# Weight tiles at 128 modulo 256 bytes, weight parts formed later, and a second layer by pairs of output chunks

## The chip, the cores and the metric

The program runs on one NeuronCore of one Trainium2 chip. The metric is the device time of one execution in microseconds; three runs of the kernel before took 576.20, 577.55 and 580.22 us (median 577.55).

## What is computed

Causal attention (2 batches, 12 heads, 448 positions, 64 wide) gives x, 896 tokens by 768. A gated layer and an output layer follow, then a second pair of layers with a cosine:

```python
x = attention(q, k, v)                      # 896 x 768
x = (sigmoid(x @ w_gate) * (x @ w_val)) @ w_out     # 768 -> 1536 -> 768
h = x @ w_in                                # 768 -> 2048
return (h * cos(h)) @ w_out2                # 2048 -> 768
```

All inputs are float32. The weights arrive as 64-bit words and are turned into float32 on the chip.

## The kernel before

**Layout.** Features stand on the 128 partitions, tokens in the free dimension, 448 (one batch) to a matmul. A weight chunk is up to six blocks of 128x128, laid out as 128x768.

**Three matmuls to a block product.** Float32 operands are split in a high and a low part (type float32r): `hi` is rounded by ScalarE (ACT), `lo` is the difference, formed by VectorE (DVE). One product of a weight block with a 448-token operand is hi by high, hi by low, lo by high (L221 to L223 in `products`, L521 to L523 in the units below). From the start of the first layer to the end these are 144 + 630 + 432 + 576 + 576 = 2358 matmuls (plain products, units, second, third and fourth layer) of the one form 128x128 by 128x448.

**A chunk's way.** DMA `wraw` (two buffers), ACT rounds the top half into `up` (L157), DVE puts the words together in `wf` (L159), ACT rounds `whi` (L169, L484), DVE subtracts `wlo` (L171, L418). Each engine works off its instructions strictly in the order in which they are written; there is no scheduler.

**First layer.** The first two feature chunks (`PLAIN`) are plain products. The other ten are units of Strassen's scheme: seven block products p1 to p7 of nine matmuls each, written in the order 1, 5, 2, 6, 4, 7, 3, where 4 belongs to the unit before. (The first unit has 1, 5, 6, 2, 7, 3, the last one's 4 follows alone.) The weights of p1 and p2 are a chunk's own parts (`A`); those of p5 and p6 are the parts of sums `s12`, those of p7 and p3 of sums `s34`, that of p4 the tile `a22`. The other operands are blocks of x and the sums T1 to T4, which are formed once, during the plain products.
Between the products stand: after p1 a copy of PSUM bank a to b (L547), over which p2 must wait, since it writes on into a; after p6 the sum c = b + s5 (L562), over which p7 must wait, since it writes on into b. `emit` writes a product first and then the work after the product before it; the weight work of the next chunk follows in each turn of the loop.
In the last unit `split_h` begins to split the layer's results h into high and low (one ACT and one DVE instruction each, L226 and L227).

**Second layer and on.** For each of six output chunks m, two weight chunks c, two batches b: 18 matmuls. `advance()` splits the next chunk, decodes the one after and loads a third. Third and fourth layer are alike; the change leaves them as they are.

**Addresses.** Tiles lie in SBUF in the order in which pools are opened and tags first used. In the built program, bytes within a partition: `wraw` at 16512, `up`, two `wf`, then four `whi` from 38048 and four `wlo` from 50336, 3072 apart; all eight are 160 modulo 256. `a22` is 224 modulo 256. Every operand that streams against them (x, T, h, y, g) is 192 modulo 256. Blocks within a tile are 512 bytes (weights) or 1792 bytes (moving) apart, so the remainder is that of every matmul of its kind, or with blocks of 512 bytes its own again.

Of the kernel before, what the change touches and what calls it, by code (L numbers as in the profile page):

```python
# [9 lines left out]
F32 = mybir.dt.float32  # L10
F32R = mybir.dt.float32r
# [4 lines left out]
AF = mybir.ActivationFunctionType  # L16
# [3 lines left out]
P = 128  # L20
B, H, S, D = 2, 12, 448, 64
# [6 lines left out]
KX = DM // P  # L28
# [3 lines left out]
WC = 6  # L32
# [3 lines left out]
WH = KP * P  # L36
PLAIN = 2
# [32 lines left out]
def attn_moe_moe2(  # L70
# [9 lines left out]
    nc = tc.nc  # L80
# [2 lines left out]

    wpool = ctx.enter_context(tc.tile_pool(name="wpool", bufs=4))
    bpool = ctx.enter_context(tc.tile_pool(name="bpool", bufs=1))
    psum = ctx.enter_context(tc.tile_pool(name="psum", bufs=8, space=PSUM))

    def bank():
        return psum.tile([P, 512], F32, tag="ps", name="ps")

    def slot(tag, name, dtype=F32R):
        pool = gpool if tag[0] == "g" else spool if tag[0] == "t" else hpool if tag in ("f0", "f1", "f2") else bpool
        return pool.tile([P, 2, S], dtype, tag=tag, name=name)
# [12 lines left out]
    chunks = []  # L106
    for f in range(KH):
        chunks.append((w_gv[f, :, 0], KX))
        chunks.append((w_gv[f, :, 1], KX))
    for m in range(KX):  # L110
        for c in range(0, KH, WC):
            chunks.append((w_out[m, :, c : c + WC], WC))
    for f in range(KG):
        chunks.append((w_in2[f], KX))
    for m in range(KX):
        for c in range(0, KG, WC):
            n = min(WC, KG - c)
            chunks.append((w_out2[m, :, c : c + n], n))
    raws, singles, parts = {}, {}, {}
# [4 lines left out]
    def step(kind):  # L124
        c = at_chunk[kind]
        at_chunk[kind] = c + 1
        return c if c < len(chunks) else None
# [13 lines left out]
    class Chunk:  # L141
# [22 lines left out]
        def split(self, step, e0, e1):  # L164
            if step == 0:
                if e0 == 0:
                    self.hi = wpool.tile([P, WC * P], F32R, tag="whi", name="whi")
                    self.lo = wpool.tile([P, WC * P], F32R, tag="wlo", name="wlo")
                nc.scalar.activation(self.hi[:, e0:e1], self.w[:, e0:e1], AF.Copy)  # L169
            else:  # L170
                nc.vector.tensor_tensor(  # L171
                    self.lo[:, e0:e1], self.w[:, e0:e1], self.hi.bitcast(F32)[:, e0:e1], op=ALU.subtract
                )
                if e1 == self.n:
                    parts[self.c] = (self.hi, self.lo)
# [15 lines left out]
    def next_chunk():  # L191
        return parts.pop(step("use"))
# [15 lines left out]
    def decode_load():  # L208
        decode_chunk()
        load_chunk()  # L210

    def advance():
        split_chunk()
        decode_load()

    def products(ps, wt, rhs, first, last, ks=None):
        hi, lo = wt
        n = len(rhs)
        for k in ks or range(n):
# [9 lines left out]
    with tc.tile_pool(name="apool", bufs=1) as apool, tc.tile_pool(name="a2", bufs=2) as a2:  # L229
# [12 lines left out]
        at = {}  # L242
# [142 lines left out]
        wt = next_chunk()  # L385
        pg = [bank()]
        xr = [[XB[b][k] for k in KORD] for b in range(B)]
# [13 lines left out]
    hpool = ctx.enter_context(tc.tile_pool(name="hpool", bufs=1))  # L401
    early = ExitStack()
    epool = early.enter_context(tc.tile_pool(name="epool", bufs=1))
    epool.tile([P, 8], F32, tag="pad", name="pad")

    def temp(tag, bufs):
        return epool.tile([P, S], F32, tag=tag, name=tag, bufs=bufs)
# [9 lines left out]
    def difference(dst, a, b):  # L417
        nc.vector.tensor_tensor(dst, a, b, op=ALU.subtract)  # L418
# [19 lines left out]
    def run(n):  # L438
        for i in range(n):
            next(todo, None)  # L440
# [3 lines left out]
    def gated(f, b, sg, val):  # L444
        if HF[f] is None:
            HF[f] = slot(f"f{f}", f"h{f}", F32)
        nc.vector.tensor_tensor(HF[f][:, b], sg, val, op=ALU.mult)

    for f in range(PLAIN):
        sg = []  # L450
        if f:
            wt = next_chunk()
            pg = []
            advance()
        else:
            decode_load()
        for b in range(B):
            if f:
                pg.append(bank())
                products(pg[b], wt, xr[b], True, True)  # L460
            sg.append(temp("sg", 4))
            nc.scalar.activation(sg[b], pg[b][:, :S], AF.Sigmoid)
            run(3)
        wt = next_chunk()
        if f == PLAIN - 1:
            words = [singles[2 * PLAIN].w]
        advance()
        if f == PLAIN - 1:
            words.append(singles[2 * PLAIN + 1].w)
        for b in range(B):  # L470
            pv = bank()
            products(pv, wt, xr[b], True, True)
            gated(f, b, sg[b], pv[:, :S])
            run(3)

    class Unit:

        def __init__(self, f):
            self.f = f

        def parts(self, src):
            hi = wpool.tile([P, WC * P], F32R, tag="whi", name="whi")
            lo = wpool.tile([P, WC * P], F32R, tag="wlo", name="wlo")
            nc.scalar.activation(hi, src, AF.Copy)  # L484
            return hi, lo

# [14 lines left out]
            difference(self.s34[:, :WH], f0[:, :WH], f1[:, :WH])  # L501
            difference(self.s34[:, WH:], f0[:, WH:], self.s12[:, WH:])

        def prepare34(self):
            self.sums34()
            self.S34 = self.parts(self.s34)
            self.low(self.S34, self.s34)

        def prepare22(self):
            t = epool.tile([P, 2, WH], F32R, tag="a22", name="a22", bufs=2)  # L510
            src = self.w[1][:, WH:]
            nc.scalar.activation(t[:, 0], src, AF.Copy)
            difference(t[:, 1], src, t.bitcast(F32)[:, 0])
            self.A22 = t[:, 0], t[:, 1]

        def product(self, ps, weights, half, rhs, first, last):
            hi, lo = weights
# [26 lines left out]
        def after(self, n):  # L544
# [18 lines left out]
            else:  # L563
# [2 lines left out]
                self.tmp = temp("tmp", 2)  # L566
                nc.vector.tensor_tensor(self.tmp, self.e[:, :S], self.s5, op=ALU.add)


    HTAGS = ["t12", "t13", "t14"] + [f"{x}{i}" for x, i0 in (  # L570
        ("b", 0), ("t", 0), ("b", 3), ("t", 3), ("t", 6), ("b", 6), ("t", 9)) for i in range(i0, i0 + 3)]
# [2 lines left out]
    H = [[None] * KH for b in range(B)]  # L574

    def split_h(n):
        for i in range(n):
            if HORD:
                k, b = HORD.pop(0)
                H[b][k] = slot(HTAG.pop(0), f"h{k}{b}")  # L580
                split(H[b][k], HF[k][:, b])

    def upper_of():
        k = Chunk(step("decode"))
        k.decode(0, 0, k.n)
        return k

    def word_of(k):
        k.decode(1, 0, k.n)
        load_chunk()  # L590
        return k.w
# [3 lines left out]
    def emit(u, n):  # L595
        u.p(n)
        if done:
            v, m = done.pop()
            v.after(m)
        done.append((u, n))  # L600

    unit, old = Unit(PLAIN), None
    unit.w, unit.A = words, next_chunk()
    unit.sums12()
    unit.S12 = unit.parts(unit.s12)
    unit.low(unit.S12, unit.s12)
    for f in range(PLAIN, KH):
        new, last = Unit(f + 1), f == KH - 1
        for at, n in enumerate((1, 5, 2, 6, 4, 7, 3) if old else (1, 5, 6, 2, 7, 3)):
            emit(old if n == 4 else unit, n)  # L610
            if at == 0:
                unit.prepare34()
            elif at == 1:
                unit.prepare22()
                k0 = upper_of()
            elif at == 2:
                w0 = word_of(k0)
                new.A = unit.parts(w0)
            elif at == 3:
                unit.low(new.A, w0)  # L620
                k1 = upper_of()
            elif at == 4:
                new.w = w0, word_of(k1)
                if not last:
                    new.sums12()
            elif at == 5 and not last:
                new.S12 = new.parts(new.s12)
                new.low(new.S12, new.s12)
            run(3)
            if last and at:  # L630
                split_h(2)
        unit, old = new, unit
    emit(old, 4)
    old.after(4)
    early.close()

# [5 lines left out]
    singles[2 * KH + 1] = k1  # L642
    X2 = [[None] * KX for b in range(B)]
    nch = KH // WC
    for m in range(KX):
        ps2 = [bank(), bank()]
        for c in range(nch):
            wt = next_chunk()
            advance()
            for b in range(B):  # L650
                products(ps2[b], wt, H[b][c * WC : c * WC + WC], c == 0, c == nch - 1)
                split_h(4)
                if c == nch - 1:
                    X2[b][m] = slot(f"f{2 * m + b}", f"y{m}{b}")
                    split(X2[b][m], ps2[b][:, :S])

    def turns(ph):
        k = tpool.tile([P, S], F32, tag="t0", name="k")  # L660
# [25 lines left out]
    for f in range(KG):  # L686
        wt = next_chunk()
# [10 lines left out]
    nch = (KG + WC - 1) // WC  # L698
    for m in range(KX):
        ps2 = [bank(), bank()]  # L700
        for c in range(nch):
            wt = next_chunk()
# [71 lines left out]
```

## Time and profile before

| | us |
|---|---|
| runs, median (lowest, highest) | 577.55 (576.20, 580.22) |
| the profiled execution, device time | 578.74 |
| its span, first to last instruction | 577.0 |
| TensorE busy | 563.9 (98%) |
| VectorE, ScalarE, GpSimd busy | 336.5, 315.6, 59.2 |

TensorE (PE) carries 94% of the chain of work that ended last. Its matmuls are pipelined: each lasts about 0.37 us in the records while a new one starts every 0.20 us, so the time of a stretch is read from the distance between starts, not from the durations. The mean granted TensorE clock is 0.991 of full. Stages: attention to about 79 us, plain products to 104.6, units to 245.9, second layer to about 335, third and fourth to 573.5.

### The profile page before, as it was taken

To read this page: it belongs to the slowest core of one execution; us is meant where nothing else is said; L and a number is where in the kernel's file an instruction comes from. 1 tells how busy PE (TensorE), PEld (TensorE's weight loads), DVE (VectorE), ACT (ScalarE), POOL (GpSimd) and SP (SyncE) were. 2 spreads that over 40 slices of the span, in tenths; PEclk is the share of its full clock that TensorE was granted. 3 is DMA by queue.
4 is the path that set the end of the run, shared out by engine and by line. 5 is a ranking of instruction groups with operands and counts; after the bars stand their busy time and mean duration, and the time that the engine had idled before them with its cause. 6 is when DMAs were issued, how large, how long until landed. Compare 5 with 4: busy or idle time off the path is not lost.

```text
span 577.0 us, 8165 instructions
## 1 busy us (share of the span) xinstructions
PE 563.9 (98%) x3104; PEld 492.4 (85%) x3104; DVE 336.5 (58%) x623; ACT 315.6 (55%) x611; POOL 59.2 (10%) x131
## 2 busy tenths in 40 slices
PE   7999999899999999799999999999999999999997
PEld 5666689699999989699999999999999999999996
DVE  5889969677777676773333337777777723311310
ACT  5899865465555555563333248777777732422320
POOL 4779830000000000000000000000000000000000
PEclk9999999899999999799999999999999999999999
DMA  8655033154443333333333313333333134532500
GB/s 331 243 182 205 2 110 111 55 160 122 136 130 110 110 110 110 110 109 110 111 109 110 110 56 109 110 109 111 109 101 96 60 115 154 176 98 99 161 33 32
DMA packets 14726, 68.15 MB, mean 118 GB/s; under 512 B 1632, under 2 KB 3808, under 8 KB 14688
## 3 DMA queue, kind: packets, MB, share of 16 engines
q1 hardware_dynamic: 14400, 67.33, 35.7%
q8 instruction: 24, 0.39, 0.3%
q10 hardware_dynamic: 288, 0.31, 0.2%
q14 instruction: 14, 0.11, 0.1%
HBM read 64.88 MB, written 2.75 MB: 117 GB/s over the span
## 4 chain that ended last, share of the span: by engine, by line
PE 94%; DVE 2%; ACT 2%; POOL 1%; issue 1%; ACTq 0%; POOLq 0%
PE ps L221 21%; PE ps L223 20%; PE ps L222 20%; PE ps L521 7%; PE ps L523 7%; PE ps L522 7%; PE ps L319 4%; PE ps L335 4%; PE ps L295 3%; POOL pbuf L279 1%; ACT pbuf L303 1%; PE ps L249 1%; ACT up L157 0%; ACT h L226 0%; DVE h L227 0%
## 5 line engine op out<-in xcount | busy, mean ns | idle before, releaser
L171 DVE TENSOR_TENSOR wlo<-wf,whi 128x768 fp32r<-128x768 f32 (+2 forms) x51 | 47.3, 928 | 64.5 <-ACT whi L169 63.5
L157 ACT ACTIVATE up<-wraw 128x768 f16<-128x768 bf16 (+2 forms) x71 | 74.0, 1043 | 10.1 <-DMA wraw<-in_w_out_dram 10.1
L159 DVE SCALAR_TENSOR_TENSOR wf<-wraw,up 128x768 uint32<-128x768 uint32 (+2 forms) x71 | 66.8, 941 | 18.0 <-ACT up L157 17.2
L222 PE MATMUL ps<-y,whi 128*128 128x448 f32 x192 | 70.9, 369 | 0.0
L222 PE MATMUL ps<-g,whi 128*128 128x448 f32 x192 | 70.9, 369 | 0.0
L221 PE MATMUL ps<-y,whi 128*128 128x448 f32 x192 | 70.8, 369 | 0.0
L223 PE MATMUL ps<-y,wlo 128*128 128x448 f32 x192 | 70.8, 369 | 0.0
L221 PE MATMUL ps<-g,whi 128*128 128x448 f32 x192 | 70.8, 369 | 0.0
L223 PE MATMUL ps<-g,wlo 128*128 128x448 f32 x192 | 70.8, 369 | 0.0
L223 PE MATMUL ps<-h,wlo 128*128 128x448 f32 x144 | 53.1, 369 | 0.0
L221 PE MATMUL ps<-h,whi 128*128 128x448 f32 x144 | 53.1, 369 | 0.0
L222 PE MATMUL ps<-h,whi 128*128 128x448 f32 x144 | 53.1, 369 | 0.0
L169 ACT ACTIVATE whi<-wf 128x768 fp32r<-128x768 f32 (+2 forms) x51 | 40.9, 803 | 15.9 <-DVE wf L159 15.9
L303 ACT ACTIVATE pbuf<-ps,nm 128x64 f32<-128x64 f32 (+6 forms) x84 | 38.6, 481 | 9.5 <-DVE nm L299 8.9
L664 DVE SCALAR_TENSOR_TENSOR r<-r,k 128x448 f32<-128x448 f32 x32 | 20.0, 625 | 35.8 <-ACT r L663 34.3
L521 PE MATMUL ps<-T,whi 128*128 128x448 f32 x90 | 34.6, 385 | 5.9 <-DVE ps L562 3.5
L279 POOL TENSOR_SCALAR pbuf<-pbuf,rs 128x64 f32<-128x64 f32 (+6 forms) x84 | 39.1, 486 | 9.4 <-PE ps L295 6.3
L221 PEld LDWEIGHTS ps<-y,whi 128*128 128x128 f32 x192 | 36.1, 188 | 3.6
L223 PEld LDWEIGHTS ps<-g,wlo 128*128 128x128 f32 x192 | 36.1, 188 | 3.6
L223 PEld LDWEIGHTS ps<-y,wlo 128*128 128x128 f32 x192 | 36.1, 188 | 3.6
L221 PEld LDWEIGHTS ps<-g,whi 128*128 128x128 f32 x192 | 36.1, 188 | 3.6
L222 PEld LDWEIGHTS ps<-g,whi 128*128 128x128 f32 x192 | 36.1, 188 | 3.5
(96 smaller groups left out, 1098.5 us busy)
## 6 DMA issues: line engine op xcount, KB each, us to landing
wraw<-in_w_gv_dram SPq DMA_DIRECT2D x24, 768.0 KB, 4.3
wraw<-in_w_out_dram SPq DMA_DIRECT2D x24, 768.0 KB, 4.4
wraw<-in_w_in_dram SPq DMA_DIRECT2D x16, 768.0 KB, 4.3
qkv<-in_qkv_dram SPq DMA_DIRECT2D x9, 928.0 KB, 5.0
wraw<-in_w_out_dram SPq DMA_DIRECT2D x6, 512.0 KB, 3.8
out_dram<-o SPq DMA_DIRECT2D x11, 224.0 KB, 2.0
qkv<-in_qkv_dram SPq DMA_DIRECT2D x3, 256.0 KB, 6.1
qkv<-in_qkv_dram SPq DMA_DIRECT2D x1, 672.0 KB, 5.7
```

The source lines that it names most:

```text
L157: nc.scalar.activation(up.bitcast(F16)[:, 1::2], self.top[:, e0:e1], AF.Copy)
L159: nc.vector.scalar_tensor_tensor(self.w[:, e0:e1].bitcast(U32), self.mid[:, e0:e1], 13, up.bitcast(U32), op0=ALU.logical_shift_right, op1= ...
L169: nc.scalar.activation(self.hi[:, e0:e1], self.w[:, e0:e1], AF.Copy)
L171: nc.vector.tensor_tensor(self.lo[:, e0:e1], self.w[:, e0:e1], self.hi.bitcast(F32)[:, e0:e1], op=ALU.subtract)
L221: mm(ps[:, :S], lhsT=hi[:, blk], rhs=r[:, 0], start=first and k == 0, stop=False)
L222: mm(ps[:, :S], lhsT=hi[:, blk], rhs=r[:, 1], start=False, stop=False)
L223: mm(ps[:, :S], lhsT=lo[:, blk], rhs=r[:, 0], start=False, stop=last and k == n - 1)
L279: nc.gpsimd.tensor_scalar(row, row, rs[:, i : i + 1], 1.0, op0=ALU.mult, op1=ALU.mult)
L303: nc.scalar.activation(pb[:, POFF[i] : POFF[i] + w], ps[:, :w], AF.Exp, scale=-1.0, bias=nm[:, i : i + 1], accum_out=sums[:, i : i + 1],)
L521: mm(ps[:, :S], lhsT=hi[:, blk], rhs=r[:, 0], start=start, stop=False, skip_group_check=True)
L522: mm(ps[:, :S], lhsT=hi[:, blk], rhs=r[:, 1], start=False, stop=False, skip_group_check=True)
L523: mm(ps[:, :S], lhsT=lo[:, blk], rhs=r[:, 0], start=False, stop=stop, skip_group_check=True)
```

## The change

Three things are done, all in one function.

**Addresses.** `whi` and `wlo` are allocated first in their pool (`first` holds the pair of the first chunk), so they start at 16512 and 28800, and the pad in front of `epool` grows from 8 to 48 floats. In the built program all `whi`, `wlo` and `a22` are then 128 modulo 256; the streamed operands stay at 192, at the addresses that they had.

**Order in the units.** The sums `s12` of the first unit, and their parts, are formed inside the last plain product; in a unit the parts of a set of sums are formed one block product behind the sums, and the high part of `a22` and the decoding of the next chunk come ahead of them; the low parts of `A` and `S12` of the next unit move to the end. The last unit splits 9 instead of 12 of the 24 tiles of h.

**Second layer.** Output chunks are done in pairs: four PSUM banks, and for each batch both chunks' weights, so that the second batch is wanted two products later.

```diff
+    def weights(tag):
+        return wpool.tile([P, WC * P], F32R, tag=tag, name=tag)
+
+    first = [weights("whi"), weights("wlo")]
...
-    for m in range(KX):
+    for m in range(0, KX, 2):
         for c in range(0, KH, WC):
-            chunks.append((w_out[m, :, c : c + WC], WC))
+            for i in range(2):
+                chunks.append((w_out[m + i, :, c : c + WC], WC))
...
-    epool.tile([P, 8], F32, tag="pad", name="pad")
+    epool.tile([P, 48], F32, tag="pad", name="pad")
...
+        def high22(self):
+            self.a22 = epool.tile([P, 2, WH], F32R, tag="a22", name="a22", bufs=2)
+            nc.scalar.activation(self.a22[:, 0], self.w[1][:, WH:], AF.Copy)
+            self.A22 = self.a22[:, 0], self.a22[:, 1]
+
+        def low22(self):
+            difference(self.a22[:, 1], self.w[1][:, WH:], self.a22.bitcast(F32)[:, 0])
...
         advance()
         if f == PLAIN - 1:
-            words.append(singles[2 * PLAIN + 1].w)
+            unit = Unit(PLAIN)
+            unit.w = words + [singles[2 * PLAIN + 1].w]
+            unit.sums12()
+            unit.S12 = unit.parts(unit.s12)
         for b in range(B):
             pv = bank()
             products(pv, wt, xr[b], True, True)
-            gated(f, b, sg[b], pv[:, :S])
+            if f == PLAIN - 1 and b == 0:
+                unit.low(unit.S12, unit.s12)
             run(3)
+            gated(f, b, sg[b], pv[:, :S])
...
             emit(old if n == 4 else unit, n)
             if at == 0:
-                unit.prepare34()
+                unit.high22()
+                k0 = upper_of()
+                unit.sums34()
             elif at == 1:
-                unit.prepare22()
-                k0 = upper_of()
+                unit.S34 = unit.parts(unit.s34)
+                unit.low22()
+                w0 = word_of(k0)
             elif at == 2:
-                w0 = word_of(k0)
-                new.A = unit.parts(w0)
+                k1 = upper_of()
+                unit.low(unit.S34, unit.s34)
             elif at == 3:
-                unit.low(new.A, w0)
-                k1 = upper_of()
+                new.A = unit.parts(w0)
+                new.w = w0, word_of(k1)
             elif at == 4:
-                new.w = w0, word_of(k1)
-                if not last:
+                if last:
+                    unit.low(new.A, w0)
+                else:
                     new.sums12()
             elif at == 5 and not last:
                 new.S12 = new.parts(new.s12)
+                unit.low(new.A, w0)
+            if at == len(order) - 1 and not last:
                 new.low(new.S12, new.s12)
             run(3)
-            if last and at:
-                split_h(2)
+            if last and at > 1:
+                split_h(1 + at // 4)
         unit, old = new, unit
     emit(old, 4)
+    split_h(1)
     old.after(4)
...
-    for m in range(KX):
-        ps2 = [bank(), bank()]
+    for m in range(0, KX, 2):
+        ps2 = [[bank() for i in range(2)] for b in range(B)]
         for c in range(nch):
-            wt = next_chunk()
-            advance()
+            wts = [next_chunk()]
             for b in range(B):
-                products(ps2[b], wt, H[b][c * WC : c * WC + WC], c == 0, c == nch - 1)
-                split_h(4)
-                if c == nch - 1:
-                    X2[b][m] = slot(f"f{2 * m + b}", f"y{m}{b}")
-                    split(X2[b][m], ps2[b][:, :S])
+                advance()
+                for i in range(2):
+                    if i and not b:
+                        wts.append(next_chunk())
+                    products(ps2[b][i], wts[i], H[b][c * WC : c * WC + WC], c == 0, c == nch - 1)
+                    split_h(3)
+                    if c == nch - 1:
+                        X2[b][m + i] = slot(f"f{2 * (m + i) + b}", f"y{m + i}{b}")
+                        split(X2[b][m + i], ps2[b][i][:, :S])
```

ScalarE before the first unit and in its first products, before the change (T is a sum of x, `s12` and `s34` sums of weights, `up` the top half of a chunk, L547 the copy of bank a to b):

```order
L157 ACTIVATE up_86<-wraw_85 128x768
L226 ACTIVATE T12_1267<-xf4_83 128x448
L226 ACTIVATE T22_1270<-xf5_84 128x448
...
L226 ACTIVATE T42_1276<-xf5_84 128x448
L484 ACTIVATE whi_1472<-s12_1469 128x768
L484 ACTIVATE whi_1489<-s34_1486 128x768
L547 COPY ps_1503<-ps_1476 128x448
L512 ACTIVATE a22_1505<-wf32_1412 128x384
L157 ACTIVATE up_86<-wraw_85 128x768
```

The same place of the changed kernel, whose lines are numbered anew (L521 is the copy of a to b):

```order
L164 ACTIVATE up_88<-wraw_87 128x768
L462 ACTIVATE whi_1419<-s12_1416 128x768
L232 ACTIVATE T12_1267<-xf4_85 128x448
...
L232 ACTIVATE T42_1276<-xf5_84 128x448
L484 ACTIVATE a22_1486<-wf32_1412 128x384
L164 ACTIVATE up_88<-wraw_87 128x768
L521 COPY ps_1503<-ps_1476 128x448
L462 ACTIVATE whi_1505<-s34_1490 128x768
```

The rounding of the parts of `s12` has moved ahead of six roundings of T, and the copy of the bank ahead of the rounding of the parts of `s34`. The later units have the same turn of the copy and the `s34` rounding.

VectorE in the last unit up to the sum c (L562), before the change:

```order
L418 TENSOR_TENSOR s34_2475<-wf32_2386,s12_2431 128x384
L418 TENSOR_TENSOR wlo_2479<-s34_2475,whi_2478 128x768
L418 TENSOR_TENSOR a22_2494<-wf32_2416,a22_2494 128x384
L227 TENSOR_TENSOR h00_2499<-h0_1320,h00_2499 128x448
L227 TENSOR_TENSOR h10_2502<-h1_1435,h10_2502 128x448
L159 SCALAR_TENSOR_TENSOR wf32_2497<-wraw_85,up_86 128x768
L227 TENSOR_TENSOR h20_2521<-h2_1585,h20_2521 128x448
L227 TENSOR_TENSOR h30_2524<-h3_1696,h30_2524 128x448
L418 TENSOR_TENSOR wlo_2519<-wf32_2497,whi_2518 128x768
L227 TENSOR_TENSOR h40_2541<-h4_1807,h40_2541 128x448
L227 TENSOR_TENSOR h50_2544<-h5_1918,h50_2544 128x448
L562 TENSOR_TENSOR ps_2556<-ps_2492,s5_2514 128x448
```

And of the changed kernel, where the sum c is L536:

```order
L424 TENSOR_TENSOR s34_2479<-wf32_2366,s12_2430 128x384
L424 TENSOR_TENSOR a22_2475<-wf32_2400,a22_2475 128x384
L166 SCALAR_TENSOR_TENSOR wf32_2477<-wraw_87,up_88 128x768
L424 TENSOR_TENSOR wlo_2495<-s34_2479,whi_2494 128x768
L233 TENSOR_TENSOR h00_2514<-h0_1324,h00_2514 128x448
L166 SCALAR_TENSOR_TENSOR wf32_2511<-wraw_87,up_88 128x768
L233 TENSOR_TENSOR h10_2533<-h1_1448,h10_2533 128x448
L536 TENSOR_TENSOR ps_2545<-ps_2492,s5_2509 128x448
```

Four splits of h and one low part of weights no longer stand ahead of the sum; one putting-together of words has come ahead of it.

## Rows read from the trace of the kernel before

**Rows 1.** Timeline of PE, plain products: start us, us, engine line op out<-in count.
```profile
79.33 0.47 PE L221 MATMUL ps<-x,whi 128*128 128x448 f32 x1
...
104.64 0.36 PE L521 MATMUL ps<-x,whi 128*128 128x448 f32 x1
```

**Rows 2.** Stages: stretch, us, busy us (instructions) of each engine, granted clock, DMA.
```profile
106.20:113.90 7.70, 4.94 (x16) 3.68 (x15) 5.44 (x10) 3.78 (x6) 0.00 (x0) 0.78 0.00 0
150.20:163.20 13.00, 13.00 (x64) 11.72 (x63) 9.40 (x15) 7.17 (x12) 0.00 (x0) 1.00 0.41 123
246.00:573.00 327.00, 327.00 (x1584) 297.48 (x1583) 149.78 (x210) 158.52 (x252) 0.00 (x0) 1.00 0.32 105
```

**Rows 3.** Timeline of PE, a unit: p2 from its first matmul.
```profile
150.18 0.46 PE L521 MATMUL ps<-x,whi 128*128 128x448 f32 x1
150.47 0.36 PE L522 MATMUL ps<-x,whi 128*128 128x448 f32 x1
...
150.88 0.37 PE L521 MATMUL ps<-x,whi 128*128 128x448 f32 x1
...
151.50 0.37 PE L521 MATMUL ps<-x,whi 128*128 128x448 f32 x1
```

**Rows 4.** Timeline of PE, another unit: p2, p6, then p4, whose weights are a22.
```profile
189.65 0.36 PE L522 MATMUL ps<-x,whi 128*128 128x448 f32 x1
...
193.06 0.36 PE L521 MATMUL ps<-T,a 128*128 128x448 f32 x1
...
193.67 0.36 PE L521 MATMUL ps<-T,a 128*128 128x448 f32 x1
```

**Rows 5.** Timeline of PE, the first unit: p1's last matmul and p5.
```profile
106.24 0.37 PE L523 MATMUL ps<-x,wlo 128*128 128x448 f32 x1
109.05 0.47 PE L521 MATMUL ps<-T,whi 128*128 128x448 f32 x1 [2.45 <-ACT whi L484]
...
111.03 0.57 PE L523 MATMUL ps<-T,wlo 128*128 128x448 f32 x1
...
113.27 0.57 PE L523 MATMUL ps<-T,wlo 128*128 128x448 f32 x1
...
113.94 0.36 PE L522 MATMUL ps<-T,whi 128*128 128x448 f32 x1
```

**Rows 6.** Timeline of PE, the last unit: p4's last matmul, p7, p3.
```profile
233.87 0.36 PE L523 MATMUL ps<-T,a 128*128 128x448 f32 x1
237.69 0.74 PE L521 MATMUL ps<-T,whi 128*128 128x448 f32 x1 [3.46 <-DVE ps L562]
...
243.71 0.36 PE L522 MATMUL ps<-x,whi 128*128 128x448 f32 x1
```

**Rows 7.** Waits: who waited for whom: us in total, times, longest us.
```profile
PEld ps L521 <- ACT ps L547: 2.1, 10, 0.3
```

**Rows 8.** Timeline of ACT around the first unit's start.
```profile
99.76 2.89 ACT L226 ACTIVATE T<-xf 128x448 fp32r<-128x448 f32 x6
108.16 0.84 ACT L484 ACTIVATE whi<-s 128x768 fp32r<-128x768 f32 x1 [5.51 <-DVE s L418]
...
111.71 0.53 ACT L547 COPY ps<-ps 128x448 f32<-128x448 f32 x1
...
112.59 1.06 ACT L157 ACTIVATE up<-wraw 128x768 f16<-128x768 bf16 x1
```

**Rows 9.** Timeline of DVE around the first unit's start.
```profile
99.92 0.96 DVE L159 SCALAR_TENSOR_TENSOR wf<-wraw,up 128x768 uint32<-128x768 uint32 x1
...
105.38 1.69 DVE L227 TENSOR_TENSOR T<-xf,T 128x448 fp32r<-128x448 f32 x3
106.98 0.55 DVE L495 TENSOR_TENSOR s<-wf 128x384 f32<-128x384 f32 x1
...
109.03 0.96 DVE L418 TENSOR_TENSOR wlo<-s,whi 128x768 fp32r<-128x768 f32 x1 [0.91 <-ACT whi L484]
```

**Rows 10.** Timeline of DVE, the last unit: the sum c.
```profile
237.01 0.63 DVE L562 TENSOR_TENSOR ps<-ps,s 128x448 f32<-128x448 f32 x1
```

More of the change, by code (lines that the diff above doesn't have):

```diff
@@ L166, in split @@
                 if e0 == 0:
-                    self.hi = wpool.tile([P, WC * P], F32R, tag="whi", name="whi")
-                    self.lo = wpool.tile([P, WC * P], F32R, tag="wlo", name="wlo")
+                    self.hi, self.lo = first if self.c == 0 else (weights("whi"), weights("wlo"))
                 nc.scalar.activation(self.hi[:, e0:e1], self.w[:, e0:e1], AF.Copy)
@@ L447, in gated @@
         nc.vector.tensor_tensor(HF[f][:, b], sg, val, op=ALU.mult)
-    for f in range(PLAIN):
-        sg = []
-        if f:
-            wt = next_chunk()
-            pg = []
-            advance()
[L455 to L468, printed above, removed]
-            words.append(singles[2 * PLAIN + 1].w)
-        for b in range(B):
-            pv = bank()
-            products(pv, wt, xr[b], True, True)
-            gated(f, b, sg[b], pv[:, :S])
-            run(3)
     class Unit:
@@ L481, in parts @@
         def parts(self, src):
-            hi = wpool.tile([P, WC * P], F32R, tag="whi", name="whi")
-            lo = wpool.tile([P, WC * P], F32R, tag="wlo", name="wlo")
+            hi, lo = weights("whi"), weights("wlo")
             nc.scalar.activation(hi, src, AF.Copy)
@@ L502, in sums34 @@
             difference(self.s34[:, WH:], f0[:, WH:], self.s12[:, WH:])
[L504 to L514, printed above, removed]
+        def high22(self):
[4 more added lines that the diff above has]
+            difference(self.a22[:, 1], self.w[1][:, WH:], self.a22.bitcast(F32)[:, 0])
         def product(self, ps, weights, half, rhs, first, last):
@@ L567, in after @@
                 nc.vector.tensor_tensor(self.tmp, self.e[:, :S], self.s5, op=ALU.add)
+    for f in range(PLAIN):
+        sg = []
+        if f:
+            wt = next_chunk()
+            pg = []
+            advance()
+        else:
+            decode_load()
+        for b in range(B):
+            if f:
+                pg.append(bank())
+                products(pg[b], wt, xr[b], True, True)
+            sg.append(temp("sg", 4))
+            nc.scalar.activation(sg[b], pg[b][:, :S], AF.Sigmoid)
+            run(3)
+        wt = next_chunk()
+        if f == PLAIN - 1:
+            words = [singles[2 * PLAIN].w]
+        advance()
+        if f == PLAIN - 1:
+            unit = Unit(PLAIN)
+            unit.w = words + [singles[2 * PLAIN + 1].w]
+            unit.sums12()
+            unit.S12 = unit.parts(unit.s12)
+        for b in range(B):
+            pv = bank()
+            products(pv, wt, xr[b], True, True)
+            if f == PLAIN - 1 and b == 0:
+                unit.low(unit.S12, unit.s12)
+            run(3)
+            gated(f, b, sg[b], pv[:, :S])
     HTAGS = ["t12", "t13", "t14"] + [f"{x}{i}" for x, i0 in (
@@ L600, in emit @@
         done.append((u, n))
[L602 to L606, printed above, removed]
+    old = None
+    unit.A = next_chunk()
     for f in range(PLAIN, KH):
         new, last = Unit(f + 1), f == KH - 1
-        for at, n in enumerate((1, 5, 2, 6, 4, 7, 3) if old else (1, 5, 6, 2, 7, 3)):
+        order = (1, 5, 2, 6, 4, 7, 3) if old else (1, 5, 6, 2, 7, 3)
+        for at, n in enumerate(order):
             emit(old if n == 4 else unit, n)
             if at == 0:
-                unit.prepare34()
+                unit.high22()
+                k0 = upper_of()
+                unit.sums34()
             elif at == 1:
-                unit.prepare22()
-                k0 = upper_of()
+                unit.S34 = unit.parts(unit.s34)
+                unit.low22()
+                w0 = word_of(k0)
             elif at == 2:
-                w0 = word_of(k0)
+                k1 = upper_of()
+                unit.low(unit.S34, unit.s34)
+            elif at == 3:
                 new.A = unit.parts(w0)
-            elif at == 3:
-                unit.low(new.A, w0)
-                k1 = upper_of()
+                new.w = w0, word_of(k1)
             elif at == 4:
-                new.w = w0, word_of(k1)
-                if not last:
+                if last:
+                    unit.low(new.A, w0)
+                else:
                     new.sums12()
@@ L644, in attn_moe_moe2 @@
     nch = KH // WC
-    for m in range(KX):
-        ps2 = [bank(), bank()]
+    for m in range(0, KX, 2):
+        ps2 = [[bank() for i in range(2)] for b in range(B)]
         for c in range(nch):
-            wt = next_chunk()
-            advance()
+            wts = [next_chunk()]
             for b in range(B):
-                products(ps2[b], wt, H[b][c * WC : c * WC + WC], c == 0, c == nch - 1)
-                split_h(4)
-                if c == nch - 1:
-                    X2[b][m] = slot(f"f{2 * m + b}", f"y{m}{b}")
-                    split(X2[b][m], ps2[b][:, :S])
+                advance()
+                for i in range(2):
[6 more added lines that the diff above has]
+                        split(X2[b][m + i], ps2[b][i][:, :S])
     def turns(ph):
```

## The prediction

> **What bounds the kernel now.** PE carries 94% of the chain that ended last, so I asked what sets the distance from one matmul to the next. I read the timeline of PE by starts (durations overlap), then the stages, then what ended its few waits.
>
> All 2358 matmuls of the four layers have one form, but three paces. In the plain products 126 start between 79.33 and 104.64 [rows 1]: 25.31 us, or 0.200 us each once the first 0.3 us are taken off. In the last three layers 1584 touch the stretch of 327.0 us, two begun before it: 327.0/1582 = 0.2067 us [rows 2]. In the units both occur: after a short wait three matmuls come 0.20 apart, then 0.62 us for three [rows 3]. And at the granted half clock six take 2.24 us, 0.373 each [rows 5]. Half of that, 0.187 us, is what streaming 448 columns would take at full clock, so 13 or 20 ns of each full-speed step are not streaming.
>
> What chooses between 0.200 and 0.2067? The weights are at 160 modulo 256 in both, so the address alone doesn't. But one stretch ran at 0.200 for 17 steps (3.41 us) and changed where weights at another remainder came, a22 at 224: 0.61 us for three from there [rows 4]. The plain products kept 0.200 until the first wait. So the slow pace is entered after a wait or a change of remainder, and once entered it stays: nothing interrupts the 1582.
>
> Two long waits stand out. The first unit's p5 waits 2.45 us for the high part of the s12 weights, then the clock falls to half for a while (0.78 on average); from 106.24 to 113.94 only 14 steps are made [rows 2, 5]. In the last unit p7 waits 3.46 us for the sum c on DVE; from 233.87 to 243.71 17 steps [rows 6]. Smaller ones: p2 of each unit waits 0.1 us for the copy of its bank [rows 3, 7].
>
> **The change part by part.** From 106.24 the trace has 7.70 us (14 steps), 119.93 us (580 steps, 113.94 to 233.87), 9.84 us (17), 2.29 us (12, to 246.0) and 327.0 us (1582) [rows 2, 5, 6]: 466.8 us for 2205 steps (counted by the program's nine matmuls to a block product). I put the changed kernel against this.
>
> *The first wait.* ACT stands idle for 5.51 us before it rounds the parts of s12, because DVE reaches the sums only at 106.98, behind six low parts of T and the gates [rows 8, 9]. In the change the sums follow the words of the chunk, which are done at 100.88: sums to 102.0 (1.15 us, as 106.98 to 108.13), high part 102.9, low part 103.9. The six roundings of T follow on ACT, 2.89 us, to 105.8; on DVE three low T (1.69 us) to 105.6, one gate (about 0.6) to 106.2, three more T to 107.9, gate 108.5. PE wants p5 at 106.44: all of its weights and T1 are there. The wait is gone, and with it the half clock, which the trace shows only behind the two long waits.
>
> What is late next: s34 sums 108.5 to 109.6 on DVE, then the low part of a22 (0.55) and the next words (0.96) to 111.1, the low part of s34 to 112.1, the sum c to 112.7 with row lengths laid end to end, 112.1 where they overlap as three T in 1.69 us do. At 0.200 a product takes 1.8 us, so p7 wants bank b at 111.84. I take 0.4 us between 0.3 and 0.9. The next unit's low part of A comes up to 0.4 us late behind the same queue; I take 0.2. New waits: **0.6 us**.
>
> *The units.* The copy now stands before the rounding that waits for the s34 sums: behind a rounding for a22 (as the copy, 0.53), the upper halves (1.06) and its own 0.53 [rows 8], some 2.7 us into the unit where p2 starts at 3.6. The nine waits of 0.1 us go. DVE is busy for 9.4 of 13.0 us and ACT for 7.2 [rows 2], with the same instructions before and after, so a unit of 63 x 0.200 = 12.6 us still covers them. S12's low part, now last, ends about 0.5 us into the unit, and p5 wants it at 1.8.
>
> *The last wait.* The sum c starts at 237.01 and p7 wanted it by 234.1 [rows 6, 10]: DVE was alternating with ACT over six splits of h and two low parts. Now two splits stand ahead. Counted from the unit's start: gate 1.3, s34 2.4, a22 3.0, words 3.9, low s34 4.9, h00 6.3 (ACT rounds it after two chunk halves, 5.7), words 7.2, h10 8.2, c 8.8 against p7 at 9.0. The wait goes; if the cover fails, tenths of a microsecond come back.
>
> *The second layer by pairs.* Matmuls, bytes and instructions are the same. The splits of h that moved out of the unit are wanted after two more products, 7.2 us. What gets tighter is a pair's second chunk: its parts stand behind the last split of the pair before, 0.55 + 0.84 + 0.96 and some signalling, 3 us where 3.6 are there. Nothing, either way; SP's queue keeps its order.
>
> *The addresses.* No trace here has weights at 128. The bounds come from the rows: at best no more than streaming, 0.187; at worst I take the slow pace and one more step of its size, 0.2133. I choose 0.200: it is the fastest pace seen at full clock, it held for as long as neither a wait nor a change of remainder came, and the change takes away the change of remainder (a22 now equals the rest) and nearly all waits.
>
> The Trainium skill speaks against it: "TensorE: Matmul & The Clock Gate", on what each phase of a matmul is for, says that PE has two independent SBUF read ports, so that loading the next weights takes no bandwidth from the running matmul, and under "Back-to-back issue gap" gives 448/2.4 + 2.5 = 189 ns, an estimate by that page. By that rule an address could neither cost nor give anything. The measured 200 and 206.7 ns, and the change of pace at a22, fit it badly; that rule without its number is rival B below.
>
> *The sum.* 2205 steps at 0.200 are 441.0 us, 25.8 less than 466.8: the two waits with their half clock 4.90 and 6.44, the units 3.93 (0.9 of it the nine waits), the rest 10.6 by pace. With 0.6 of new waits 25.2 go. The profiled execution took 578.74 us (span 577.0), 1.2 above the median of the runs; 578.74 - 25.2 = 553.5, and 552.4 at the level of the median.
>
> **The rivals.**
> *B, the pace stays as it is.* The new wait of the first unit sends PE into 0.2067, as most waits in the units did, and the addresses don't bring it back: 2205 x 0.2067 = 455.7, 11.1 less, 0.6 back: 577.55 - 10.5 = **567.0**. For it: at one remainder both paces exist. A mixture ends between, near 560.
> *C, the pace falls below 0.200.* One step of 6.7 ns less on the 2339 steps from 79.33 is another 15.6 us: **536.8**; no overhead at all would be 521. For it: at half clock nothing but the stream is seen. Against it: nothing at full clock has been faster than 0.200.
> *D, slower: the new remainder is worse.* If weights at 128 collide more often with the stream at 192, at 0.2133, the time is 567.0 + 0.9 (the plain products lose their fast pace) + 15.6 = **583.5**. It decides from 0.2108 on, where 552.4 + 2339 x 0.0108 reaches the old time. For it: the remainder does move the pace [rows 4], and no row shows this one.
> *E, a new long wait.* Should one of my orders be late by what the old ones were, 4.9 to 6.4 us come back: about 558 on top of my forecast, 573 on top of B. Against it: the margins above fall short by tenths at most.
>
> **How the numbers follow.** My forecast 0.45, B with mixtures 0.28, C 0.17, D 0.06, E 0.04. The time is that of the likeliest, 552.4. The range reaches to C's first step and to B: 535 to 569; outside stay D, the rest of C and part of E, under 2 in 10. The likeliest case alone spans 550 to 555. About 1%, 5.8 us, is what a measurement can tell from no change: faster by more (under 571.8) 0.89, within 0.06, slower 0.05.
>
> **What would show it.** In the profile after: steps of 0.200 from 79 us to the end, and 316 us for 1582 of them; no half clock behind p5 of the first unit or p7 of the last; p2 starting without a pause; DVE's sum c of the last unit ending before p7 is due. Steps of 0.2067 in the second layer would make me wrong by B, 0.193 by C, 0.213 by D; a new idle stretch of microseconds by E.

## The result, and the profile after

The changed kernel took **553.5 us** (median of 4 runs, 553.38 to 553.67) against 577.83 us (4 runs, 576.20 to 580.22) of the kernel before: a ratio of 0.9576, 95% interval 0.9542 to 0.9610. Forecast were 552.4 us, range 535 to 569. The profiled execution took 553.42 us, 25.3 us less than that of the kernel before; 25.2 were forecast.

The page of the changed kernel, its span and two of its parts: busy us (share) and instructions of PE, and the granted clock in 40 slices of the span.

```profile
span 551.6 us, 8156 instructions
...
PE 544.9 (99%) x3104; PEld 488.4 (89%) x3104; DVE 334.4 (61%) x623; ACT 315.1 (57%) x611; POOL 59.2 (11%) x131
...
PEclk9999999999999999999999999999999999999999
```

PE is busy for 19 us less with the same 3104 instructions, and no slice of the clock stands below 9. The stages, with the columns of [rows 2]:

```profile
106.20:113.90 7.70, 7.70 (x39) 6.92 (x38) 7.54 (x13) 4.70 (x7) 0.00 (x0) 1.00 0.32 98
113.90:233.80 119.90, 119.90 (x599) 111.86 (x599) 92.19 (x140) 74.29 (x117) 0.00 (x0) 1.00 0.40 126
...
250.00:540.00 290.00, 290.00 (x1452) 271.88 (x1451) 137.24 (x191) 147.01 (x233) 0.00 (x0) 1.00 0.33 109
```

In the first line, where the kernel before had 16 matmuls at a mean clock of 0.78, there are 39 at full clock. In the last, 1452 matmuls touch 290.0 us, two of them begun before it: 290.0/1450 = 0.2000 us a step, against 0.2067 in the same layers before.

The timeline of PE shows where the changed kernel still waits (start us, us, engine line op out<-in count; p7 of the first unit, p1 of the second, p4 of the last):

```profile
79.17 0.47 PE L227 MATMUL ps<-x,whi 128*128 128x448 f32 x1
...
111.49 0.37 PE L497 MATMUL ps<-x,wlo 128*128 128x448 f32 x1
111.82 0.47 PE L495 MATMUL ps<-T,whi 128*128 128x448 f32 x1
...
115.73 0.37 PE L496 MATMUL ps<-x,whi 128*128 128x448 f32 x1
116.03 0.47 PE L497 MATMUL ps<-x,wlo 128*128 128x448 f32 x1
...
116.74 0.36 PE L497 MATMUL ps<-x,wlo 128*128 128x448 f32 x1
...
228.94 0.37 PE L497 MATMUL ps<-x,wlo 128*128 128x448 f32 x1
229.23 0.47 PE L495 MATMUL ps<-T,a 128*128 128x448 f32 x1
...
547.74 0.37 PE L229 MATMUL ps<-g,wlo 128*128 128x448 f32 x1
```

The last matmul of the kernel before:

```profile
573.09 0.37 PE L223 MATMUL ps<-g,wlo 128*128 128x448 f32 x1
```

From 79.17 to 547.74 there are 2339 steps in 468.57 us, where the kernel before needs 493.8 for as many (79.33 to 573.09). At 0.200 a step they would take 467.80; the rest is 0.1 at the start and the three waits, which with the two or three longer steps behind them cost 0.24, 0.21 and 0.20 us. Behind each the pace returns to 0.200: the 561 steps from 116.74 to 228.94 take 112.20 us, with nine p4 in between. This answers [rows 3] and [rows 4], where the pace stayed at 0.2067 behind a wait or changed at a p4.

The long waits are gone [rows 5, 6]. ACT around the start of the first unit, against [rows 8]:

```profile
101.96 0.84 ACT L462 ACTIVATE whi<-s 128x768 fp32r<-128x768 f32 x1 [2.21 <-DVE s L424]
102.71 2.90 ACT L232 ACTIVATE T<-xf 128x448 fp32r<-128x448 f32 x6
...
106.88 0.55 ACT L521 COPY ps<-ps 128x448 f32<-128x448 f32 x1
```

The high part of s12 is rounded at 101.96, 6.2 us earlier, and the copy of the bank ends at 107.43, before p6 (108.1) writes on. DVE in the first unit and in the last (L536 is the sum c, L541 the sum after p7):

```profile
110.27 0.95 DVE L424 TENSOR_TENSOR wlo<-s,whi 128x768 fp32r<-128x768 f32 x1
111.13 0.63 DVE L536 TENSOR_TENSOR ps<-ps,s 128x448 f32<-128x448 f32 x1
...
224.48 0.63 DVE L536 TENSOR_TENSOR ps<-ps,s 128x448 f32<-128x448 f32 x1
...
227.48 1.16 DVE L233 TENSOR_TENSOR h<-h,h 128x448 fp32r<-128x448 f32 x2
228.55 0.62 DVE L541 TENSOR_TENSOR tmp<-ps,s 128x448 f32<-128x448 f32 x1
```

In the first unit c ends at 111.76, just after p7 was due (111.69): the first of the three waits. In the last unit c starts at 224.48 instead of 237.01 [rows 10], in time. The sum after p7 stands behind two splits of h and ends at 229.17, when p4 was due at 229.14: the third wait.

### The profile page after: what moved, and what is told of

It is laid out like the page before. It is cut to its first block, busy times and chain, and to the rows that moved or that the text cites. A ratio compares the mean times of both kernels' runs of the same rounds, so it can differ in the third digit from the quotient of the medians.

```text
span 551.6 us, 8156 instructions
## 1 busy us (share of the span) xinstructions
PE 544.9 (99%) x3104; PEld 488.4 (89%) x3104; DVE 334.4 (61%) x623; ACT 315.1 (57%) x611; POOL 59.2 (11%) x131
## 4 chain that ended last, share of the span: by engine, by line
PE 97%; POOL 1%; ACT 1%; DVE 1%; issue 0%; ACTq 0%; DVEq 0%; POOLq 0%
PE ps L227 21%; PE ps L229 21%; PE ps L228 21%; PE ps L497 8%; PE ps L495 8%; PE ps L496 8%; PE ps L325 4%; PE ps L341 4%; PE ps L301 3%; POOL pbuf L285 1%; ACT pbuf L309 1%; PE ps L255 1%; DVE ps L305 0%; DVE rs L282 0%; POOL sums L281 0%
## 5 line engine op out<-in xcount | busy, mean ns | idle before, releaser
L227 PE MATMUL ps<-y,whi 128*128 128x448 f32 x192 | 69.7, 363 | 0.0
L227 PE MATMUL ps<-g,whi 128*128 128x448 f32 x192 | 69.7, 363 | 0.0
L229 PE MATMUL ps<-g,wlo 128*128 128x448 f32 x192 | 69.6, 362 | 0.0
L229 PE MATMUL ps<-y,wlo 128*128 128x448 f32 x192 | 69.6, 362 | 0.0
L228 PE MATMUL ps<-y,whi 128*128 128x448 f32 x192 | 69.1, 360 | 0.0
L228 PE MATMUL ps<-g,whi 128*128 128x448 f32 x192 | 69.1, 360 | 0.0
L227 PE MATMUL ps<-h,whi 128*128 128x448 f32 x144 | 52.3, 363 | 0.0
L228 PE MATMUL ps<-h,whi 128*128 128x448 f32 x144 | 51.8, 360 | 0.0
L228 PEld LDWEIGHTS ps<-y,whi 128*128 128x128 f32 x192 | 35.9, 187 | 2.5
L227 PEld LDWEIGHTS ps<-y,whi 128*128 128x128 f32 x192 | 36.0, 188 | 2.0
```

## The experiments

Two things were mixed in the gain, order and addresses, so the first two runs take one each. Two theories: **A**, the addresses set the pace; **W**, they do nothing, and the pace stayed at 0.200 because there was hardly a wait left to lose it at.

**The new order with the old addresses.**

```diff
-    first = [weights("whi"), weights("wlo")]
...
-                    self.hi, self.lo = first if self.c == 0 else (weights("whi"), weights("wlo"))
+                    self.hi, self.lo = weights("whi"), weights("wlo")
...
-    epool.tile([P, 48], F32, tag="pad", name="pad")
+    epool.tile([P, 8], F32, tag="pad", name="pad")
```

> The changed kernel with the addresses of before: the weight tiles whi and wlo at 160 and a22 at 224 modulo 256 again, everything else as changed. Theory A (the addresses set the pace: at 160 against 192 the slow pace is entered after a wait and stays): steps of 0.2067 us from the first unit's short wait on, 2205 of them 455.7 us instead of 441.0, so about 14 us slower than the changed kernel, 567 us. Theory W (the addresses do nothing, the pace stayed at 0.200 because nearly all waits are gone): as the changed kernel, 553.5 us, the same step behind every wait.

Three executions took 567.51, 567.99 and 568.12 us; the fourth, which was profiled, 557.49. The granted clock was 0.999 or 1.000 in all four, so it doesn't make the difference. So the order alone ends near rival B most of the time, and not always at the same place. The stages of the profiled execution show why (columns as in [rows 2]):

```profile
125.00:230.00 105.00, 105.00 (x512) 95.78 (x511) 76.64 (x116) 61.07 (x94) 0.00 (x0) 1.00 0.39 121
250.00:540.00 290.00, 290.00 (x1451) 272.15 (x1451) 137.32 (x191) 147.50 (x234) 0.00 (x0) 1.00 0.34 111
```

In the units 105.0/510 = 0.206 us a step, in the last layers 290.0/1449 = 0.200. The slow pace was there from the plain products on (177 steps of 0.2067 from 80.2) and ended in the last p4, whose weights at 224 come just ahead of the second layer (behind the nine earlier p4 it had come back):

```profile
233.41 0.37 PE L494 MATMUL ps<-T,a 128*128 128x448 f32 x1
...
235.04 0.36 PE L496 MATMUL ps<-T,a 128*128 128x448 f32 x1
235.24 0.36 PE L226 MATMUL ps<-h,whi 128*128 128x448 f32 x1
235.44 0.36 PE L227 MATMUL ps<-h,whi 128*128 128x448 f32 x1
235.64 0.36 PE L228 MATMUL ps<-h,wlo 128*128 128x448 f32 x1
```

W falls: ahead of the first wait, 0.2067 already occurs. At these addresses both paces are possible. The three executions near 568 were not profiled; that they kept 0.2067 to the end is worked out from their time (553.5 + 2205 x 0.0067 = 568.2), and what decides between the paces stays open.

**The new addresses with the old order.**

```diff
+    first = [wpool.tile([P, WC * P], F32R, tag=t, name=t) for t in ("whi", "wlo")]
     psum = ctx.enter_context(tc.tile_pool(name="psum", bufs=8, space=PSUM))
...
-    epool.tile([P, 8], F32, tag="pad", name="pad")
+    epool.tile([P, 48], F32, tag="pad", name="pad")
```

> The kernel before with the addresses of the change alone: whi, wlo and a22 at 128 modulo 256, moving operands at 192, order and second layer as before. Theory A: 0.200 us a step everywhere, also behind the waits, while the two long waits with their half clock (4.9 and 6.4 us) and the nine waits of p2 (0.1 to 0.2 us each) stay: 441.0 + 4.9 + 6.4 + 1.4 = 453.7 instead of 466.8 us, so about 564.5 us. Theory W: the pace falls to 0.2067 behind the same waits as before, 577.5 us.

565.32 us (564.89 to 566.00, 4 runs; ratio to before 0.9803, 0.9743 to 0.9863), 9.6 us less than the 574.9 of the kernel before in the same series: faster, though the interval doesn't settle whether by 2%. One p2 with its wait, then the last layers:

```profile
124.53 0.37 PE L527 MATMUL ps<-T,wlo 128*128 128x448 f32 x1
124.84 0.47 PE L525 MATMUL ps<-x,whi 128*128 128x448 f32 x1
125.15 0.36 PE L526 MATMUL ps<-x,whi 128*128 128x448 f32 x1
125.34 0.37 PE L527 MATMUL ps<-x,wlo 128*128 128x448 f32 x1
125.55 0.36 PE L525 MATMUL ps<-x,whi 128*128 128x448 f32 x1
125.75 0.36 PE L526 MATMUL ps<-x,whi 128*128 128x448 f32 x1
```

```profile
250.00:540.00 290.00, 290.00 (x1452) 271.81 (x1451) 141.51 (x198) 148.05 (x236) 0.00 (x0) 1.00 0.35 113
```

A holds: all the waits of before, and 0.200 behind each of them. A wait costs not only its own 0.1 us but as much again in the step after it (124.53 to 125.15 is 0.62 for two), 0.2 us in all.
The two long waits and their half clock are here as before:

```profile
110.06 0.47 PE L525 MATMUL ps<-T,whi 128*128 128x448 f32 x1 [2.45 <-ACT whi L488]
...
236.64 0.53 PE L525 MATMUL ps<-T,whi 128*128 128x448 f32 x1 [3.58 <-DVE ps L566]
236.97 0.57 PE L526 MATMUL ps<-T,whi 128*128 128x448 f32 x1
...
240.33 0.37 PE L526 MATMUL ps<-x,whi 128*128 128x448 f32 x1
```

The first is for the high part of s12, the second for the sum c, and the nine steps from 236.97 take 3.36 us, 0.373 each. So the order is worth 565.3 - 553.5 = 11.8 us at the new addresses.

**What about the addresses?** Two theories again: **D**, the distance of the moving operand from the weights modulo 256 decides (64 in the changed kernel, 32 before); **R**, the weights' own remainder does. The pad in front of the moving operands, or one in front of all, moves them apart (the pad of `epool` keeps a22 with the other weights).

```diff
-    bpool.tile([P, 8], F32, tag="pad", name="pad")
...
-    epool.tile([P, 48], F32, tag="pad", name="pad")
+    epool.tile([P, 56], F32, tag="pad", name="pad")
```

> The changed kernel with all moving operands 32 bytes lower: weights at 128, moving operands at 160 modulo 256, so 32 apart as in the kernel before (160 and 192). If the distance of the two decides (theory D), the slow pace of 0.2067 us comes behind the first wait and stays: 567 us. If the weights' own remainder decides (theory R: 128 is a multiple of 64, 160 is not), 0.200 us a step and 553.5 us.

567.15 us, and 290.0/1403 = 0.2067 us a step in the last layers (second line; the first is of the units):

```profile
113.90:233.80 119.90, 119.90 (x587) 109.52 (x587) 89.68 (x137) 71.10 (x111) 0.00 (x0) 1.00 0.41 128
250.00:540.00 290.00, 290.00 (x1405) 263.79 (x1405) 135.13 (x188) 146.06 (x230) 0.00 (x0) 1.00 0.33 108
```

The time came as theory D has it, the place did not: the units ran at a third pace, 119.9/585 = 0.205 us a step with the one wait in it, the plain products too, and 0.2067 came only in the last p4, far behind that wait.

```diff
+    wpool.tile([P, 8], F32, tag="wpad", name="wpad", bufs=1)
     first = [weights("whi"), weights("wlo")]
```

> The changed kernel with everything 32 bytes higher: weights at 160, where the kernel before has them, moving operands at 224, so 64 apart as in the changed kernel. Theory D (the distance decides): 0.200 us a step, 553.5 us. Theory R (the weights' own remainder decides): 0.2067 us a step behind the first wait, 567 us.

553.60 us, 290.0/1450 = 0.200:

```profile
250.00:540.00 290.00, 290.00 (x1452) 271.87 (x1451) 137.42 (x191) 147.11 (x234) 0.00 (x0) 1.00 0.33 109
```

D holds and R falls, both ways: weights at 128 with a distance of 32 are slow, weights at 160 with 64 are fast. These are one execution each. The distance of the moving operands from the tiles `wraw`, `up` and `wf` is no rival: in the built programs it is the same in the kernel before and in the changed one. Four more distances, by the pad in front of the moving operands (16, 24, 40 and 56 floats; the pad of `epool` keeps a22 at 128). The edit for 0 modulo 256:

```diff
-    bpool.tile([P, 8], F32, tag="pad", name="pad")
+    bpool.tile([P, 24], F32, tag="pad", name="pad")
...
-    epool.tile([P, 48], F32, tag="pad", name="pad")
+    epool.tile([P, 32], F32, tag="pad", name="pad")
...
-        k = tpool.tile([P, S], F32, tag="t0", name="k")
+        k = tpool.tile([P, S], F32, tag="t0", name="k", bufs=1)
...
```

> The changed kernel with the moving operands at 224 modulo 256, 96 above the weights at 128. If only the distance of 64 is free of the slow pace (theory N), 0.2067 us a step behind a wait, 567 us. If any distance of 64 or more will do (theory M), 0.200 us a step, 553.5 us. Should a larger distance leave less between two streams, 0.1933 us a step and 538 us.

> The changed kernel with the moving operands at 0 modulo 256, 128 above the weights at 128 (to make room, the temporaries of the third layer and of the outputs have one buffer instead of two, off PE's path). Theory N: 0.2067 us a step or more, 567 us or more. Theory M: 0.200 us, 553.5 us.

> The changed kernel with the moving operands at 64 modulo 256, 192 above the weights at 128 (one buffer for the temporaries of the third layer and the outputs). Theory N: 0.2067 us a step or more, 567 us or more. Theory M: 0.200 us, 553.5 us.

> The changed kernel with the moving operands at 128 modulo 256, as the weights (one buffer for the temporaries of the third layer and the outputs). Distance 0 is further from 64 than the 32 of the kernel before. Theories N and M: the slow pace or a slower one, 0.2067 to 0.2133 us a step from the start, 567 to 584 us.

565.66, 562.87, 558.73 and 559.65 us, one execution each. The last layers of the four, in this order:

```profile
250.00:540.00 290.00, 290.00 (x1414) 265.07 (x1413) 135.08 (x188) 145.69 (x230) 0.00 (x0) 1.00 0.34 110
```

```profile
250.00:540.00 290.00, 290.00 (x1424) 267.00 (x1423) 135.75 (x189) 147.30 (x233) 0.00 (x0) 1.00 0.33 109
```

```profile
250.00:540.00 290.00, 290.00 (x1436) 268.84 (x1435) 137.35 (x191) 147.57 (x234) 0.00 (x0) 1.00 0.33 109
```

```profile
250.00:540.00 290.00, 290.00 (x1432) 268.80 (x1432) 137.34 (x191) 147.72 (x234) 0.00 (x0) 1.00 0.33 109
```

| moving minus weights, modulo 256 | mean step in the last layers, us (290 us / matmuls less two) | time, us |
|---|---|---|
| 0 | 0.2028 | 559.65 |
| 32 | 0.2067 (in the order-only run 0.200) | 567.15 |
| 64 | 0.2000 | 553.5, 553.60 |
| 96 | 0.2054 | 565.66 |
| 128 | 0.2039 | 562.87 |
| 192 | 0.2022 | 558.73 |

Theory M (64 or more will do) falls; N holds in that only 64 was free of the longer steps in every run, but not in its sizes: the others are slower by 2 to 7 ns, most in patterns of three to five step lengths that repeat, and a distance of 0 is among the better ones, not the worst. The moving operand's own remainder doesn't decide either: at 224 it is fast with weights at 160 (553.60) and slow with weights at 128 (565.66). At 0, 96, 128 and 192 there is one execution each; whether they scatter as 32 does is not known. None has a mean below 0.200 or above 0.2067, so rivals C and D have no distance among the six tried.

**a22 alone at its old remainder.**

```diff
-    epool.tile([P, 48], F32, tag="pad", name="pad")
+    epool.tile([P, 8], F32, tag="pad", name="pad")
```

> The changed kernel with only the pad in front of epool as before, so a22 is at 224 modulo 256 (the nine matmuls of each p4, 90 in all) and all other weights at 128. If a weight tile at another distance disturbs the pace for itself alone: 90 steps off 0.200 by up to 6.7 ns, at most 0.6 us, 553.5 to 554.1 us. If it sets the pace of what follows, as in the kernel before: 0.2067 us behind the first p4, up to 14 us more.

554.09 us. One p4 of it, whose nine steps take 1.83 instead of 1.80 us, and the return to 0.200:

```profile
123.28 0.37 PE L495 MATMUL ps<-T,a 128*128 128x448 f32 x1
...
125.11 0.36 PE L495 MATMUL ps<-T,whi 128*128 128x448 f32 x1
125.31 0.36 PE L496 MATMUL ps<-T,whi 128*128 128x448 f32 x1
125.51 0.36 PE L497 MATMUL ps<-T,wlo 128*128 128x448 f32 x1
```

A tile at another distance (224 here) sets no pace for what follows, if the others are 64 apart. The ten p4 cost 0.3 us by this; the time is 0.6 above the changed kernel's, in one execution of another series.

**The second layer without pairs.**

```diff
...
+            wt = next_chunk()
+            advance()
...
+                products(ps2[b], wt, H[b][c * WC : c * WC + WC], c == 0, c == nch - 1)
+                split_h(5)
...
```

> The changed kernel with the second layer as before, one output chunk at a time (five splits of h behind each product, since 15 are left over from the units). If the pairs are worth nothing by themselves: 553.5 us, and no wait of PE in the second layer. If the splits that moved out of the last unit need the room of a pair: waits for h at the start of the second layer, one to several us more.

553.52 us (553.33 to 553.73, 4 runs), as the changed kernel. The pairs are worth nothing by themselves; the splits that left the last unit are in time without them.

**The last three waits taken away.**

```diff
             elif at == 2:
                 k1 = upper_of()
-                unit.low(unit.S34, unit.s34)
+                if old:
+                    unit.low(unit.S34, unit.s34)
             elif at == 3:
+                if not old:
+                    unit.low(unit.S34, unit.s34)
...
                     new.sums12()
+                    if not old:
+                        unit.low(new.A, w0)
             elif at == 5 and not last:
                 new.S12 = new.parts(new.s12)
-                unit.low(new.A, w0)
+                if old:
+                    unit.low(new.A, w0)
...
-                split_h(1 + at // 4)
+                split_h((1, 1, 2, 1, 3)[at - 2])
```

> The changed kernel with its last three waits taken away by order alone: in the first unit the sum c ahead of the low part of s34 and the low part of A ahead of the sum after p7; in the last unit one split of h instead of two ahead of that sum. The trace of the changed kernel loses 0.24, 0.21 and 0.20 us at them beyond 0.200 us a step: 552.9 us, if nothing else comes late; 553.5 if they reappear a place further on.

553.03 us (552.67 to 553.07, 5 runs), below every run of the changed kernel. PE now goes from the start of the plain products to the last layer without a pause:

```profile
79.81 0.36 PE L227 MATMUL ps<-x,whi 128*128 128x448 f32 x1
...
523.61 0.36 PE L229 MATMUL ps<-g,wlo 128*128 128x448 f32 x1
...
547.00 0.37 PE L229 MATMUL ps<-g,wlo 128*128 128x448 f32 x1
```

Up to 523.61 those are 2219 steps in 443.80 us, 0.2000 each, and the pace stays the same to the last matmul. In the two profiled executions the waits account for the gain: the 2339 steps take 467.91 us instead of 468.57, 0.66 less, where 0.65 was lost at the waits. The medians differ by 0.5 us, with runs up to 0.4 us apart. What is left in the matmuls is the step itself.

## Why the prediction was right

**The sum.** 25.2 us were to go, and the stretch from 79 us to the last matmul is 25.2 us shorter (493.8 to 468.6); the span is 551.6 against 551.8 reckoned. 553.5 against 552.4 is the step from the profiled execution to the median: before, the profiled execution lay above the median of the shown runs by 1.2 us; after, it lies with them. The parts agree too: the waits and their half clock were put at 4.90 + 6.44 + 0.9 - 0.6 = 11.6 us, and the order is worth 11.8 at the new addresses.

**The pace.** 0.200 was chosen as the fastest pace seen at full clock. It held, in all 2339 steps but those behind three waits. The reason given was half right. Right: the address matters, which the trace of before showed at a22 [rows 4]. Wrong was the step "the slow pace is entered after a wait or a change of remainder, and once entered it stays": in the order-only run the slow pace was there from the first plain products and ended at a p4. The trace of before already spoke against it, in the unit of [rows 4]:

```profile
188.53 0.37 PE L523 MATMUL ps<-T,wlo 128*128 128x448 f32 x1
...
189.15 0.37 PE L523 MATMUL ps<-T,wlo 128*128 128x448 f32 x1
189.35 0.46 PE L521 MATMUL ps<-x,whi 128*128 128x448 f32 x1
```

Ahead of the wait of p2 three steps take 0.62 us, behind it the 17 steps of [rows 4] take 0.200 each: there a wait ended the slow pace. What counts is the distance between the two operands: at 32 a stretch may run at either pace (or at 0.205), at 64 it comes back to 0.200 by itself. So fewer waits and one remainder for all weights, the reasons given for 0.200, were not what brought it: the addresses-only run keeps the waits and the run with a22 alone keeps the change of remainder, and both come back to 0.200, while at a distance of 32, with few waits and one remainder, 0.2067 came. What the rows of before couldn't tell is which distance is the good one: of the six tried, only 64 gives what was forecast. That the change has 64 was luck, as far as the prediction's reasons go.

**The first wait.** Its mechanism and ledger held: low part of s12 due 103.9, ended 103.8; p5 without a wait, no half clock. New waits: 0.4 and 0.2 us put down, 0.24 and 0.21 measured.

**The last wait.** c was in time, as reckoned. Not reckoned was the same hazard one product later: p4 of the last unit writes on into the bank that the sum after p7 reads, and two splits of h stand ahead of that sum, 0.20 us.

**The units.** The nine waits went. They were put at 0.1 us each, 0.9 in all, by their own length, as the single long step of [rows 3] shows it (150.18 to 150.47); at the new addresses they would have cost 0.2 us each, by the addresses-only run.

**The second layer.** Nothing, as forecast; shown by the run without pairs.

**The rivals.** B is what order alone gives, by their time, in three executions of four. C and D found no distance. E did not come: the longest new wait cost 0.24 us. The rule of the Trainium skill ("TensorE: Matmul & The Clock Gate", "Step-by-step: what each phase is for") that loading weights takes no SBUF bandwidth from the running matmul sits badly with these runs: with nothing but pads changed, the mean step goes from 0.200 to 0.2067 us. No run shows where the longer step is lost, so that it is lost in reading SBUF is not shown. The estimate of 189 ns for 448 columns by the same page of the Trainium skill (its formula for an isolated gap, under "Back-to-back issue gap") is not reached at any distance here.

**What is open.** Why 64, and why several step lengths alternate elsewhere, no trace here tells; a distance of 160, and steps finer than 32 bytes, were not tried, and 224 occurs only where a22 keeps its old remainder (1.83 us for the nine steps of a p4, 0.2033 each). The kernels at 0, 128 and 192 had one buffer less for some temporaries; PE had no wait in the layers that use them.

## What to carry to other kernels

When equal matmuls start at unequal distances in one trace, list them by starts and by SBUF address before anything else: here some 14 us of 577 lay in 6.7 ns a step, which no busy share shows (PE stood at 98%). A wait of PE is worth the steps behind it, and the clock after a long one, more than its own length: 2.5 and 3.5 us of idling cost some 11 us here (4.90 and 6.44 in the trace of before). Order and addresses come apart only when each is run alone: 568 (or 557) and 565 us, both together 553.5.

## What the runs showed of the hardware

That the distance between weights and moving operand modulo 256 bytes shifts a float32r step of 448 columns between 0.2000 and 0.2067 us, with weights reloaded for every matmul. That at a distance of 32 the same program runs at either pace, and its time scatters: 557.5 to 568.1 us with the new order, at a clock of 0.999 or 1.000 throughout, but 553.4 to 553.7 for the changed kernel. The runs of the kernel before lie between 573.3 and 580.2 us; there the granted clock differs too (0.991 to 0.999), and how much of that is the pace is not shown. And that at half clock the step is 0.373 us for 448 columns in the kernel before and with the new addresses alike, so the extra 13 to 20 ns belong to full clock.
